# A planned order for the first 14 pairs of an attention and feed-forward kernel

## The chip, the cores and the metric

One core of one Trainium2 chip. The metric is the device time of one execution in microseconds, median of three runs.

## What is computed

Attention with a sliding window and a few sink columns, in 4 batches of 8 heads, 768 rows, head size 64; its output (3072 x 512) goes through a feed-forward layer of width 2048. Inputs are float32 (the weights arrive as 8-byte floats).

```python
scores = scale * np.matmul(q, k.transpose(0, 1, 3, 2))
keep = is_sink | in_window            # pos < n_sink, or 0 <= i - j < window
scores = np.where(keep, scores, -1000000000.0)
a = softmax(scores)                   # with 1e-9 added to the sum
x = (a @ v), heads side by side       # 3072 x 512
h = x @ w_in
g = h * np.clip(h + 3.0, 0.0, 6.0) / 6.0
out = g @ w_out
```

## The kernel before

The rows of a batch are cut into three blocks of 256 (u = 0, 1, 2). A *unit* is one block of one batch, all heads; there are 12, and the four with u = 0 come first. A *pair* is two heads of a unit, so four pairs make a unit and there are 48 (index s). Pairs 0 to 11 (`plain`, NF32 = 12) are multiplied in float32; from pair 12 on each operand is split into a high and a low float32r part.

A pair goes through these steps: `A_kq`, `A_v` load keys, queries and values (SP's queue); `C_score` multiplies on TensorE (PE) into four PSUM banks (tile `sp`); `C_mask` on VectorE (DVE) adds the mask and takes the row minimum (four cells, narrow 128 and wide 256 columns, into tile `Ph`, minimum in `nb`); `C_exp` on ScalarE (ACT) makes exponentials and row sums (four cells); `C_sum` inverts the sums; `C_norm` multiplies each cell by them; `D_pt` transposes on PE (tile `pt`), `D_out` copies the result to `pf` on ACT; `E_av` multiplies by the values on PE (tile `av`); `E_out` splits the result into `xh` (ACT) and `xl` (DVE).

The feed-forward layer of a unit needs its four pairs. It has 32 steps on PE: `ffn1` (L534) for each of 8 column blocks i and two halves, 12 matmuls into `hps`; `ffn2` (L564) for each i and two row tiles, 6 matmuls into `o`. Between them ACT makes the relu, DVE the product, ACT or DVE the high part `gh` and DVE the low part `g`. The weights come in 32 parts of 512 KB (`load_part`, L134): a load on SP's queue, two ACT operations and two DVE operations that turn 8-byte floats into 4-byte ones (tiles `st`, `wt`), then the high part on ACT (`wih`, `woh`) and the low part on DVE (`wil`, `wol`). Three `st` buffers and one `vs` buffer hold loaded parts.

The program has two halves. In the loop over `range(FROM)` (L667, FROM = 14) each turn s issues the steps of the string ORDER for pairs s, s-1 and s-2, some weight parts (WN), and feed-forward steps (`drain`) as far as the weights have come; the framework orders each engine's instructions there. From L717 on the order is written by hand (`manual_schedule`, the strings STAGES): each turn runs eight stages of a pair, and after each stage one feed-forward step. `keep_busy` (L77) issues matmuls without use, 50 calls in all, each two instructions in the trace.

Ahead of the pairs DVE makes the masks from `n_sink` and `window`, which are loaded by two small DMAs (L87, L88), in a chain of thirteen operations (L90 to L121); `later_constants` (L183) makes the masks for u > 0 on GpSimd (POOL).

The normalisation alternates (NORM0 = "DADA": narrow cells on DVE, wide cells on ACT); the high part of a weight is always on ACT (WHI = "A").

Of the kernel before, what the change touches and what calls it, by code (L numbers as in the profile page):

```python
# [18 lines left out]
P = 128  # L19
# [4 lines left out]
WARM = (10, 16, 4)  # L24
# [20 lines left out]
def attn_ffn_kernel(ctx: ExitStack, tc: tile.TileContext, qx, kx, vx, vfx, vsx, n_sink, window, w_in, w_out, out):  # L45
# [14 lines left out]

    rel = work.tile([P, 2, 256], F32, tag="gf", name="rel", bufs=2)
# [21 lines left out]
    keep_busy(WARM[0])  # L83
# [23 lines left out]
    own, prev, snk = relf[:, P:2 * P], relf[:, 2 * P:3 * P], colf[:, P:2 * P]  # L107
    tmpm = colf[:, 2 * P:3 * P]
    nc.vector.tensor_scalar(out=own, in0=relf[:, 0:P], scalar1=win_f, scalar2=None, op0=ALU.is_lt)
    nc.vector.scalar_tensor_tensor(out=own, in0=relf[:, 0:P], scalar=0.0, in1=own, op0=ALU.is_ge, op1=ALU.mult)  # L110
    nc.vector.tensor_scalar(out=prev, in0=relf[:, 0:P], scalar1=float(P), scalar2=win_f, op0=ALU.add, op1=ALU.is_lt)
    nc.vector.tensor_scalar(out=snk, in0=colf[:, 0:P], scalar1=ns_f, scalar2=None, op0=ALU.is_lt)

    def bias_from(dst, keep, engine=nc.vector):
        engine.tensor_scalar(out=dst, in0=keep, scalar1=-1.0, scalar2=BIG, op0=ALU.add, op1=ALU.mult)

    nc.vector.tensor_tensor(out=tmpm, in0=own, in1=snk, op=ALU.max)
    bias_from(m_00, tmpm)
    nc.vector.tensor_tensor(out=tmpm, in0=prev, in1=snk, op=ALU.max)
    bias_from(m_01[:, 0:P], tmpm)  # L120
    bias_from(m_01[:, P:2 * P], own)  # L121

# [6 lines left out]
    WHI, WLO = "A", "D"  # L129
# [4 lines left out]
    def load_part(hi, lo, src, rows, at):  # L134

        def like(t):
            return t.rearrange("p (a b) -> p a b", a=rows)

        if not wide:
            st = like(work.tile([P, 512], F32, tag="st", name="st", bufs=3))  # L140
            nc.sync.dma_start(out=st, in_=src)
            split_parts(nc, hi, lo, st, nc.scalar, nc.vector)
            return

        tag, bufs = ("vs", 1) if at % 4 == 3 else ("st", 3)
        st = work.tile([P, 512, 2], I32, tag=tag, name="st", bufs=bufs)
        it = work.tile([P, 512], I32, tag="wt", name="wt", bufs=3)
        nc.sync.dma_start(out=like(st.rearrange("p n w -> p (n w)")), in_=src.bitcast(I32))
        low, high = st[:, :, 0], st[:, :, 1]
        ft = it.bitcast(F32)  # L150


        nc.scalar.activation(out=ft, in_=high.bitcast(F32), func=AF.Abs, scale=2.0 ** -112)  # L153

        nc.scalar.activation(out=low, in_=low.bitcast(U32), func=AF.Copy, scale=2.0 ** -29 * (1 - 2.0 ** -18),  # L157
                             bias=7.5 * 2.0 ** -18 - 0.5)
        nc.vector.scalar_tensor_tensor(out=low, in0=high, scalar=-2 ** 31, in1=low,  # L159
                                       op0=ALU.bitwise_and, op1=ALU.bitwise_or)  # L160
        nc.vector.scalar_tensor_tensor(out=it, in0=it, scalar=3, in1=low,
                                       op0=ALU.logical_shift_left, op1=ALU.bitwise_or)
        copy_r(nc, weng(WHI, at), hi, like(ft))
        weng(WLO, at).tensor_tensor(out=lo, in0=like(ft), in1=hi.bitcast(F32), op=ALU.subtract)

    def load_w_in(i, c):
        cs = slice(2 * c, 2 * c + 2)
        load_part(WIH[i][:, cs, :], WIL[i][:, cs, :], w_in[i, :, cs, :], 2,
                  4 * i + c)

    def load_w_out(i, c):
        cs = slice(c, c + 1)
        load_part(WOH[i][:, cs, :], WOL[i][:, cs, :], w_out[i, :, cs, :], 1,
                  4 * i + 2 + c)


# [6 lines left out]
    def later_constants():  # L183

        bias_from(m_t0[:, 0:P], prev, nc.gpsimd)
        bias_from(m_t0[:, P:2 * P], own, nc.gpsimd)
        bias_from(m_t0[:, 2 * P:W2], snk[:, 0:SK], nc.gpsimd)
# [39 lines left out]
    NF32 = 12  # L227
    PFE = "AA"
# [13 lines left out]
    def A_v(s, planned=False):  # L242
# [13 lines left out]
        if not planned:  # L256
            A_split(s)
# [44 lines left out]
    PTAGS = [("pl", 2), ("pl", 2), ("Pt", 1)]  # L302

# [6 lines left out]
    def C_score(s, planned=False):  # L310
# [4 lines left out]
        if not plain(s):  # L315
            d["P"] = work.tile([P, 2, 2, WP], F32, name="Pt", bufs=1)
        d["sp"] = []
        for t, (k0c, w, m) in enumerate(spans(u)):
# [12 lines left out]
            if not planned:  # L331
                C_mask(s, t)
        if u and not planned:
            merge(s)

    def C_mask(s, t):
# [4 lines left out]
        for g in range(2):  # L341
            i = 2 * g + t
            if t == 0 and plain(s):
                tag, bufs = PTAGS[(2 * s + g) % len(PTAGS)]
                d[f"P{g}"] = work.tile([P, 3 * P], F32, tag=tag, name="Ph", bufs=bufs)
            d["min"] = nc.vector.tensor_tensor_reduce(out=cell(s, g, t, 0, w), in0=sp[g][:, 0:w], in1=m[:, 0:w],  # L346
                                                      scale=-SCALE, scalar=3.0e38, op0=ALU.add, op1=ALU.min,
                                                      accum_out=d["nb"][:, i:i + 1])
# [7 lines left out]
    NORM0, NORM = "DADA", "AAAA"  # L356

    def norm(e, blk, c):
        if e == "A":
            nc.scalar.mul(out=blk, in_=blk, mul=c)  # L360
        elif e == "D":
            nc.vector.tensor_scalar(out=blk, in0=blk, scalar1=c, scalar2=None, op0=ALU.mult)
        else:
            nc.gpsimd.tensor_scalar(out=blk, in0=blk, scalar1=c, scalar2=1.0, op0=ALU.mult, op1=ALU.mult)

# [3 lines left out]
    def C_exp(s, planned=False):  # L369
        d = st_[s]  # L370
        for i in range(4):
            blk = cell(s, i // 2, i % 2, *live(s)[i % 2])
            d["exp"] = nc.scalar.activation(out=blk, in_=blk, func=AF.Exp, scale=-1.0,  # L373
                                            bias=d["nb"][:, i:i + 1], accum_out=d["sm"][:, i:i + 1])
        if not planned:
            C_sum(s)
# [6 lines left out]
    def C_norm(s, planned=False):  # L383
        u = pus[s][1]
        d = st_[s]
        for i in range(4):
            blk = cell(s, i // 2, i % 2, *live(s)[i % 2])
            norm((NORM0 if s < START else NORM)[i], blk, d["rc"][:, i:i + 1])
        if not planned:
            C_sinks(s)  # L390
# [11 lines left out]
    def D_pt(s, h, planned=False):  # L402
# [12 lines left out]
        if not planned:  # L415
            D_part(s, h)
            D_out(s, h)
            if h == 1:
                D_sinks(s)
# [11 lines left out]
    def D_out(s, h):  # L431
        u = pus[s][1]
        d = st_[s]
        w = 4 * P if u else 3 * P
        pt = d[f"pt{h}"]
        if plain(s):
            ph = work.tile([P, 512], F32, tag="ph", name="pf")
            copy_r(nc, {"D": nc.vector, "A": nc.scalar}[PFE[h]], ph[:, 0:w], pt[:, 0:w])
            d[f"pt{h}"] = ph
            return  # L440
        ph = work.tile([P, 512], F32R, name="ph")
        pl = work.tile([P, 512], F32R, name="pl")
        split_parts(nc, ph[:, 0:w], pl[:, 0:w], pt[:, 0:w], nc.scalar, nc.vector)
# [9 lines left out]
    def E_av(s, h, planned=False):  # L453
# [34 lines left out]
        if h == 1:  # L488
            E_x(s)
            if not planned:  # L490
                E_out(s)
# [9 lines left out]
    def E_out(s):  # L501
        b, u, p = pus[s]
        d = st_[s]
        xh, xl = xt[(b, u)][p]
        if plain(s):
            acc = d["av"][:, 0, :]
            copy_r(nc, weng(XHF, p), xh, acc)
            nc.vector.tensor_tensor(out=xl, in0=acc, in1=xh.bitcast(F32), op=ALU.subtract)  # L508
            return
        for h in range(2):  # L510
            E_low(s, h)
            E_sum(s, h)
        E_split(s)
# [20 lines left out]
    def ffn1(x, i, pool, psum, half, state, tag):  # L534
# [12 lines left out]
        if half == 1:  # L547
# [5 lines left out]
            def activate():  # L553
                nc.scalar.activation(out=gf, in_=hp, func=AF.Relu, bias=three, scale=1.0)  # L554
# [363 lines left out]
```

## Time and profile before

| | us |
|---|---|
| median of 3 runs (722.68 to 724.12) | 723.58 |
| the profiled execution | 722.53 |
| its span, first to last instruction | 720.8 |

| engine | busy us | share of the span |
|---|---|---|
| PE, matmuls | 707.2 | 98% |
| PEld, weight loads | 626.3 | 87% |
| DVE | 504.5 | 70% |
| ACT | 451.4 | 63% |
| POOL | 5.0 | 1% |

Times are microseconds from the start of the span. A busy PE is not a PE at full flow: matmuls overlap, and the time from one start to the next tells more than the busy time. PEclk is the clock granted to TensorE, 1.00 being full. 49.45 MB are moved in the span.

### The profile page before, as it was taken

The page shows a single profiled execution, that of the slowest core. Times are in us where ns is not written, and L with a number is a line of the kernel's source. Part 1 is how long each engine was busy: PE and PEld are TensorE (multiplying, and loading weights), DVE is VectorE, ACT ScalarE, POOL GpSimd, SP SyncE. Part 2 cuts the span into 40 slices and gives each one's busy share as a digit, 9 for nine tenths or more (in the row PEclk, how much of TensorE's full clock was granted, in tenths as well). Part 3 has the DMA queues.
Part 4 walks back from the last instruction along what each step waited for, and adds up shares of the span by engine and source line. Part 5 has one row for each costly group of instructions (what it writes and reads, how often), then busy time and mean ns, then how long its engine had stood idle before and what let it go on. Part 6 is the DMA issues. An engine that isn't in the chain of part 4 may idle for free.

```text
span 720.8 us, 13229 instructions
## 1 busy us (share of the span) xinstructions
PE 707.2 (98%) x4948; PEld 626.3 (87%) x4948; DVE 504.5 (70%) x1322; ACT 451.4 (63%) x1179; POOL 5.0 (1%) x19
## 2 busy tenths in 40 slices
PE   8999999999999999999999999999999999999996
PEld 7777897889889898989898989898988898889995
DVE  5799997346578777877777777777777777775221
ACT  6999886447657656665666566656665665655222
POOL 2000000000000000000000000000000000000000
PEclk9999999999999999999999999999999999999999
DMA  6667561110211111112112111100121101100000
GB/s 240 194 199 238 188 206 61 52 52 1 64 31 60 42 49 60 31 59 68 30 31 85 35 38 60 60 32 30 60 66 32 60 30 61 60 13 1 30 1 35
DMA packets 29481, 49.45 MB, mean 69 GB/s; under 512 B 3552, under 2 KB 20448, under 8 KB 29408
## 3 DMA queue, kind: packets, MB, share of 16 engines
q1 hardware_dynamic: 29264, 48.51, 20.9%
q8 instruction: 41, 0.67, 0.4%
q14 instruction: 32, 0.26, 0.1%
q10 hardware_dynamic: 144, 0.00, 0.0%
HBM read 42.21 MB, written 6.29 MB: 67 GB/s over the span
## 4 chain that ended last, share of the span: by engine, by line
PE 89%; ACT 6%; DVE 3%; DMA 1%; issue 1%; ACTq 0%; DVEq 0%; SPq 0%
PE o L572 37%; PE hps L545 36%; PE av L486 7%; PE sp L329 6%; PE pt L410 3%; ACT Ph L373 2%; ACT wt L153 1%; ACT Ph L360 1%; ACT pf L35 1%; ACT st L157 1%; DMA raw<-in_n_sink_dram 1%; DMA st<-in_w_out_dram 1%; DVE st L159 1%; PE spt L412 1%; ACT wih L35 0%
## 5 line engine op out<-in xcount | busy, mean ns | idle before, releaser
L545 PE MATMUL hps<-xh,wih 128*128 128x256 f32 x768 | 222.5, 290 | 2.0 <-ACT wih L35 1.4
L545 PE MATMUL hps<-xh,wil 128*128 128x256 f32 x768 | 217.0, 283 | 0.0
L545 PE MATMUL hps<-xl,wih 128*128 128x256 f32 x768 | 216.5, 282 | 0.1
L572 PE MATMUL o<-woh,gh 128*128 128x512 f32 x384 | 156.1, 407 | 1.3 <-DVE gh L41 1.3
L572 PE MATMUL o<-woh,g 128*128 128x512 f32 x384 | 151.6, 395 | 0.0
L572 PE MATMUL o<-wol,gh 128*128 128x512 f32 x384 | 151.1, 393 | 0.0
L545 PEld LDWEIGHTS hps<-xh,wih 128*128 128x128 f32 x768 | 144.8, 189 | 3.7 <-ACT wih L35 1.7
L545 PEld LDWEIGHTS hps<-xl,wih 128*128 128x128 f32 x768 | 145.0, 189 | 0.9 <-DVE xl L508 0.3
L545 PEld LDWEIGHTS hps<-xh,wil 128*128 128x128 f32 x768 | 144.7, 188 | 0.8 <-DVE nb L346 0.7
L35 ACT ACTIVATE ph<-pm 128x512 fp32r<-128x512 f32 x64 | 40.5, 632 | 108.5 <-DVE pm L427 108.5
L555 DVE SCALAR_TENSOR_TENSOR gf<-gf,hps 128x512 f32<-128x512 f32 x96 | 65.7, 684 | 55.0 <-ACT gf L554 54.6
L554 ACT ACTIVATE gf<-hps,three 128x512 f32<-128x512 f32 x96 | 65.6, 683 | 56.5 <-PE hps L545 56.4
L559 DVE TENSOR_TENSOR g<-gf,gh 128x512 fp32r<-128x512 f32 x96 | 66.4, 691 | 37.6 <-ACT gh L35 35.1
L572 PEld LDWEIGHTS o<-woh,gh 128*128 128x128 f32 x384 | 72.2, 188 | 18.4 <-issue 3.3
L572 PEld LDWEIGHTS o<-woh,g 128*128 128x128 f32 x384 | 72.1, 188 | 17.8 <-DVE g L559 0.7
L572 PEld LDWEIGHTS o<-wol,gh 128*128 128x128 f32 x384 | 72.4, 189 | 11.3 <-issue 0.3
L30 DVE TENSOR_TENSOR pl<-pm,ph 128x512 fp32r<-128x512 f32 x64 | 44.3, 692 | 44.7 <-ACT ph L35 44.7
L35 ACT ACTIVATE gh<-gf 128x512 fp32r<-128x512 f32 x80 | 50.1, 626 | 26.1 <-DVE gf L555 25.9
L373 ACT ACTIVATE Pt<-Pt,nb 128x144 f32<-128x144 f32 (+2 forms) x144 | 58.7, 409 | 2.2 <-DVE nb L346 1.0
L519 ACT COPY tmp<-av 64x256 f32<-64x256 f32 x72 | 26.5, 368 | 35.6 <-PE av L486 35.1
L346 DVE CUSTOM_DVE_ANT_0 Pt<-sp,m_t 128x272 f32<-128x272 f32 x128 | 48.5, 435 | 0.0
L360 ACT ACTIVATE Pt<-Pt,rc 128x144 f32<-128x144 f32 (+2 forms) x144 | 48.2, 408 | 0.5 <-DVE rc L381 0.5
(99 smaller groups left out, 979.3 us busy)
## 6 DMA issues: line engine op xcount, KB each, us to landing
st<-in_w_in_dram SPq DMA_DIRECT2D x16, 512.0 KB, 3.9
st<-in_w_out_dram SPq DMA_DIRECT2D x16, 512.0 KB, 4.7
kr<-in_kx_dram SPq DMA_DIRECT2D x32, 200.0 KB, 2.6
qr<-in_qx_dram SPq DMA_DIRECT2D x48, 128.0 KB, 2.8
out_dram<-ost SPq DMA_DIRECT2D x24, 256.0 KB, 2.2
vr<-in_vx_dram SPq DMA_DIRECT2D x32, 192.0 KB, 2.4
VF<-in_vfx_dram SPq DMA_DIRECT2D x12, 256.0 KB, 3.4
kr<-in_kx_dram SPq DMA_DIRECT2D x16, 128.0 KB, 3.1
```

The lines of the kernel that those rows point to most:

```text
L30: lo_engine.tensor_tensor(out=lo, in0=src, in1=hi.bitcast(F32), op=ALU.subtract)
L35: nc.scalar.mul(out=out, in_=src, mul=scale)
L329: nc.tensor.matmul(out=sp[g][:, 0:w], lhsT=l[gs], rhs=r[gs], start=(j == 0), stop=(j == len(terms) - 1))
L346: d["min"] = nc.vector.tensor_tensor_reduce(out=cell(s, g, t, 0, w), in0=sp[g][:, 0:w], in1=m[:, 0:w], scale=-SCALE, scalar=3.0e38, op0=AL ...
L360: nc.scalar.mul(out=blk, in_=blk, mul=c)
L373: d["exp"] = nc.scalar.activation(out=blk, in_=blk, func=AF.Exp, scale=-1.0, bias=d["nb"][:, i:i + 1], accum_out=d["sm"][:, i:i + 1])
L486: nc.tensor.matmul(out=o, lhsT=l, rhs=r, start=(j == 0 and (h == 0 or not plain(s))), stop=(j == len(seq) - 1 and (h == 1 or not plain(s))))
L545: nc.tensor.matmul(out=hp[:, half, :], lhsT=l, rhs=r, start=(j == 0), stop=(j == n - 1))
L554: nc.scalar.activation(out=gf, in_=hp, func=AF.Relu, bias=three, scale=1.0)
L555: nc.vector.scalar_tensor_tensor(out=gf, in0=gf, scalar=6.0, in1=hp, op0=ALU.min, op1=ALU.mult)
L559: eng(GLO, state["n"] * NP).tensor_tensor(out=g, in0=gf, in1=gh.bitcast(F32), op=ALU.subtract)
L572: nc.tensor.matmul(out=acc, lhsT=l[:, f, ts_], rhs=r[i][:, f, :], start=(i == 0 and f == 0 and j == 0), stop=(i == NFP - 1 and f == 1 and ...
```

## The change

A planner runs while the program is built. `first_tasks` lists all work of pairs 0 to 13 (C, D and E up to pair 12, or 11 for E), of the 32 weight parts and of the feed-forward steps of units 0 and 1 as tasks with an engine, a cost, what they wait for, a due number and the buffers that they take and give. `in_order` lets four engines choose, each time one is free, the ready task with the lowest due number for which buffers are there; the order that comes out is issued as it is, with all four engines under `manual_schedule` from the start of the program. Tasks of engine `"*"` go to ACT or DVE, whichever is free first: the normalisations `n`, the high parts of weights `wh` and of activations `h`. Where PE has nothing and the plan's time is below QUIET, one matmul without use (`idle`) is put in. After the plan the loop over STAGES goes on from pair 14 as before, with `A_kq(14)` and unit 2 queued.

The mask chain prepares a position tile that needs no loaded value ahead of the loads, keeps the biases themselves, and has seven operations behind the loads; both small loads are now on ACT's queue. Even pairs put both heads' cells in one `Pt` tile, odd ones in two `pl` tiles (before they went round over three).

```diff
+PART_DUE = (5.4, 14.1, 33.8, 61.6, 65.3, 70.3, 72.6, 72.7, 75.9, 78, 80, 86.7, 102.5, 103.4, 105.5, 115, 115.2, 116.3,
+            118.3, 119.3, 120.2, 122.7, 123.4, 124.1, 124.2, 124.4, 141.9, 161.5, 187.6, 205, 220.3, 236.5)
+LEAD = {"kq": 39.1, "v": 38.1, "w": 38.8}
+QUIET = 30.0
+ROOM = {"kq": 2, "V": 2, "vr": 1, "split": 1, "bank": 7, "pl": 2, "Pt": 1, "ph": 2, "st": 3, "vs": 1, "wt": 3, "gf": 2,
+        "gh": 2, "x0": 2, "x1": 2, "x2": 2, "x3": 2}
+def first_tasks():
+    def add(name, eng, cost, after, due, takes=(), gives=(), lag=0.12):
+    add("mask", "DVE", 5.0, [], -100)
+    for s in range(PAIRS):
+        d = 10 * s
+        add(f"kq{s}", "SP", 0.95, [], d - LEAD["kq"], ("kq",))
+        add(f"v{s}", "SP", 0.47, [], d - LEAD["v"], ("V",) if f32 else ("V", "vr"))
...
+        hold = ("pl", "pl") if f32 and s % 2 else ("Pt",)
+        add(f"C{s}", "PE", 0.8 if f32 else 1.0, start, d, ("bank",) * 4 + hold, ("kq",) if f32 else ("split",), 0.35)
+        for t in range(2):
+            for h in range(2):
+                add(f"t{s}.{t}{h}", "DVE", 0.345 if t else 0.21, [f"C{s}", "mask"], d + 0.1, (), ("bank",))
+                add(f"x{s}.{t}{h}", "ACT", 0.49 if t else 0.385, [f"t{s}.{t}{h}"], d + 0.2)
+        add(f"c{s}", "DVE", 0.41, [f"x{s}.{t}{h}" for t in range(2) for h in range(2)], d + 0.3, lag=0.1)
+        for h in range(2):
+            for t in range(2):
+                add(f"n{s}.{t}{h}", "*", (0.41, 0.27) if t else (0.3, 0.2), [f"c{s}"], d + 0.4 + 0.01 * h)
+            add(f"D{s}.{h}", "PE", 0.4, [f"n{s}.0{h}", f"n{s}.1{h}"] + [f"D{s}.0"] * h, d + 0.5,
...
+        if f32:
+            add(f"E{s}.0", "PE", 0.68, [f"o{s}.0", f"v{s}"], d + 0.7, ("bank", f"x{s % 4}"), ("ph",))
+            add(f"E{s}.1", "PE", 0.68, [f"o{s}.1", f"E{s}.0"], d + 0.7, (), ("ph", "V"))
...
+    for k in range(32):
+        d = PART_DUE[k]
+        add(f"w{k}", "SP", 0.47, [], d - LEAD["w"], (room,))
+        add(f"wa{k}", "ACT", 0.56, [f"w{k}"], d + 0.1, ("wt",))
...
+        add(f"wh{k}", "*", (0.54, 0.336), [f"wd{k}"], d + 0.4)
+        add(f"wl{k}", "DVE", 0.605, [f"wh{k}"], d + 0.5, (), ("wt",))
+    for n in range(2):
+        for i in range(8):
+            d = 1000 + 100 * n + 5 * i
+            add(f"F{n}.{i}.0", "PE", 1.42, xs + before + [f"wl{4 * i}", f"wl{4 * i + 1}"], d, ("bank",))
+            add(f"r{n}.{i}", "ACT", 0.57, [f"F{n}.{i}.1"], -50, ("gf",))
...
+            add(f"G{n}.{i}.0", "PE", 1.4, before + [f"g{n}.{i}", f"wl{4 * i + 2}", f"wl{4 * i + 3}"], d + 1.5,
...
-    nc.sync.dma_start(out=raw[:, 1, :], in_=window.bitcast(I32).partition_broadcast(P))
+    nc.scalar.dma_start(out=raw[:, 1, :], in_=window.bitcast(I32).partition_broadcast(P))
-    rawf = const.tile([P, 2, 2], F32, name="rawf")
-    nc.vector.tensor_copy(out=rawf, in_=raw)
...
+    own = m_01[:, P:2 * P]
+    beyond(own, causal, win_f)
+    or_sink(m_00, own)
+    beyond(ahead, shifted, win_f)
+    or_sink(m_01[:, 0:P], ahead)
+    beyond(m_t0[:, 2 * P:W2], colf[:, 0:SK], ns_f)
...
+    PLAN[0] = "tasks"
+    later_constants()
+    for name, e, _ in in_order(first_tasks()):
+        do(name, e)
+    A_kq(FROM)
+    ffn_queue(2)
+    PLAN[0] = "steps"
+    for s in range(FROM, NS + 2):
+        for steps in STAGES:
+            stage(s, steps)
             drain(1)
             tick()
```

## Rows read from the trace of the kernel before

**Rows 1.** Busy time by stretch: length; PE, PEld, DVE, ACT, POOL; PEclk, DMA, GB/s.
```profile
8.40:66.75 58.35, 52.95 (x354) 42.99 (x352) 49.62 (x162) 56.95 (x159) 0.19 (x1) 1.00 0.69 219
66.75:159.05 92.30, 91.26 (x576) 79.17 (x576) 65.59 (x149) 63.04 (x140) 0.95 (x1) 1.00 0.36 116
159.05:714.90 555.85, 555.85 (x3979) 497.46 (x3978) 386.00 (x996) 329.53 (x879) 0.00 (x0) 1.00 0.13 43
```

**Rows 2.** Timeline of PE at 159 us: start, length, engine, line, operation, tiles.
```profile
159.07 0.96 PE L329 MATMUL sp<-kt,qt 64*128 64x128 f32 x12
```

**Rows 3.** PE's instructions by line, 0 to 159.05 us: count, busy, mean ns, idle before.
```profile
L545 PE MATMUL hps<-xh,wih 128*128 128x256 f32 x132 | 38.2, 291 | 2.0 <-ACT wih L35 1.4 <-ACT xh L35 0.7
...
L572 PE MATMUL o<-woh,gh 128*128 128x512 f32 x64 | 26.7, 417 | 1.3 <-DVE gh L41 1.3
```

**Rows 4.** Chain of work, PE at full flow: start, length, what.
```profile
115.70 2.85 PE hps L545 x24
...
119.21 2.79 PE o L572 x12
```

**Rows 5.** Timeline of PE, 62 to 65 us: one run of D, C, E.
```profile
62.11 0.82 PE L410 MATMUL pt<-ident_r,Ph 128*128 128x128 f32 x6
62.86 0.93 PE L329 MATMUL sp<-kr,qr 64*128 64x128 f32 x8
63.71 1.57 PE L486 MATMUL av<-pf,VF 128*128 128x256 f32 x8
65.05 0.36 PE L545 MATMUL hps<-xh,wih 128*128 128x256 f32 x1
```

**Rows 6.** PE's instructions by line, 0 to 31 us.
```profile
L81 PE MATMUL idle<-rel 128*128 128x128 f32 x100 | 14.3, 306 | 1.1 <-POOL rel L65 1.1
L486 PE MATMUL av<-pf,VF 128*128 128x256 f32 (+1 forms) x31 | 6.7, 342 | 0.0
L329 PE MATMUL sp<-kr,qr 64*128 64x128 f32 (+1 forms) x40 | 5.6, 354 | 0.1
L410 PE MATMUL pt<-ident_r,Ph 128*128 128x128 f32 x24 | 4.2, 289 | 1.3 <-DVE Ph L362 1.2
```

**Rows 7.** PE's instructions by line, 31 to 66.75 us.
```profile
L545 PE MATMUL hps<-xh,wih 128*128 128x256 f32 x28 | 8.5, 303 | 2.0 <-ACT wih L35 1.4 <-ACT xh L35 0.7
...
L486 PE MATMUL av<-pf,VF 128*128 128x128 f32 (+1 forms) x35 | 6.7, 331 | 0.0
L329 PE MATMUL sp<-kr,qr 64*128 64x128 f32 (+1 forms) x32 | 5.4, 363 | 0.6 <-ACT pf L35 0.6
L572 PE MATMUL o<-woh,gh 128*128 128x512 f32 x10 | 4.1, 409 | 1.3 <-DVE gh L41 1.3
```

**Rows 8.** Chain of work to 125 us: DVE and ACT on it.
```profile
4.90 0.18 DVE rawf L90
...
8.17 0.06 DVE Ph L346
...
20.00 1.75 ACT Ph L373 x8
...
22.27 0.91 ACT Ph L360 x2
...
28.46 0.27 ACT xh L35
28.73 0.81 ACT pf L35 x2
...
45.19 0.33 DVE gh L41
...
54.25 0.52 ACT wih L35
...
103.78 0.61 DVE wt L161
```

**Rows 9.** Waits of SP's queue: waiter, releaser, us, times, longest.
```profile
SPq L148 <- DVE wt L161: 44.4, 23, 5.4
```

More of the change, by code (lines that the diff above doesn't have):

```diff
@@ new lines, in in_order @@
+def in_order(tasks):
+    room = dict(ROOM)
+    engines = ("PE", "ACT", "DVE", "SP")
+    free = dict(PE=5.5, ACT=2.9, DVE=1.0, SP=0.8)
+    then = {name: [] for name in tasks}
+    left, at = {}, {}
+    for name, task in tasks.items():
+        left[name] = len(task[2])
+        at[name] = 0.0
+        for a in task[2]:
+            then[a].append(name)
+    coming = [(0.0, k, name) for k, name in enumerate(tasks) if not left[name]]
+    heapq.heapify(coming)
+    freed, marks, order, ready = [(QUIET, 0, ("bank",))], sorted({QUIET, *free.values()}), [], []
+    count, wire = len(tasks), 0.0
+    while marks:
+        now = heapq.heappop(marks)
+        while marks and marks[0] <= now + 1e-9:
+            heapq.heappop(marks)
+        while coming and coming[0][0] <= now + 1e-9:
+            ready.append(heapq.heappop(coming)[2])
+        while freed and freed[0][0] <= now + 1e-9:
+            for r in heapq.heappop(freed)[2]:
+                room[r] += 1
+        moved = True
+        while moved:
+            moved = False
+            for k, e in enumerate(engines):
+                if free[e] > now + 1e-9:
+                    continue
+                best = None
+                for name in ready:
+                    task = tasks[name]
+                    if task[0] == e or (task[0] == "*" and 1 <= k <= 2):
+                        if all(room[r] >= task[4].count(r) for r in task[4]) and (best is None or task[3] < tasks[best][3]):
+                            best = name
+                if best is None:
+                    if k == 0 and now < QUIET and not any(tasks[n][0] == "PE" and t < now + 0.25 for t, _, n in coming):
+                        order.append(("idle", e, now))
+                        free[e] = now + 0.224
+                        heapq.heappush(marks, free[e])
+                    continue
+                _, cost, _, _, takes, gives, lag = tasks[best]
+                ready.remove(best)
+                for r in takes:
+                    room[r] -= 1
+                cost = cost if isinstance(cost, float) else cost[k - 1]
+                free[e] = end = now + cost
+                order.append((best, e, now))
+                if e == "SP":
+                    wire = max(wire, now + (2.8 if now < 4.5 else 1.5)) + (1.6 if best[0] == "w" else 0.8)
+                    end, lag = wire + 0.7, 0.1
+                count += 1
+                if gives:
+                    heapq.heappush(freed, (end, count, gives))
+                    heapq.heappush(marks, end)
+                heapq.heappush(marks, free[e])
+                for nxt in then[best]:
+                    left[nxt] -= 1
+                    at[nxt] = max(at[nxt], end + lag)
+                    if not left[nxt]:
+                        count += 1
+                        heapq.heappush(coming, (at[nxt], count, nxt))
+                        heapq.heappush(marks, at[nxt])
+                moved = True
+    assert {o[0] for o in order} >= set(tasks), [n for n in tasks if n not in {o[0] for o in order}][:20]
+    return order
@@ L58, in attn_ffn_kernel @@
     ps = fast.enter_context(tc.tile_pool(name="ps", bufs=8, space=PSUM))
+    ET = mybir.EngineType
+    fixed = ExitStack()
+    fixed.enter_context(tc.manual_schedule(engines={ET.PE, ET.Activation, ET.DVE, ET.SP}))
     rel = work.tile([P, 2, 256], F32, tag="gf", name="rel", bufs=2)
@@ L136, in like @@
         def like(t):
             return t.rearrange("p (a b) -> p a b", a=rows)
+        tag, bufs = ("vs", 1) if k % 4 == 3 else ("st", 3)
+        if wide:
+            st = work.tile([P, 512, 2], I32, tag=tag, name="st", bufs=bufs)
+            nc.sync.dma_start(out=like(st.rearrange("p n w -> p (n w)")), in_=src.bitcast(I32))
+        else:
+            st = work.tile([P, 512], F32, tag=tag, name="st", bufs=bufs)
+            nc.sync.dma_start(out=like(st), in_=src)
+        parts[k] = (hi, lo, like, st)
@@ L240, in A_kq, with A_v @@
         st_[s].update(kr=kr, qr=qr)
-    def A_v(s, planned=False):
+    def A_v(s):
         b, u, p = pus[s]
@@ L316, in C_score @@
             d["P"] = work.tile([P, 2, 2, WP], F32, name="Pt", bufs=1)
+        elif s % 2:
+            d["P0"], d["P1"] = (work.tile([P, 3 * P], F32, tag="pl", name="Ph") for h in range(2))
+        else:
+            both = work.tile([P, 2, 3 * P], F32, tag="Pt", name="Ph", bufs=1)
+            d["P0"], d["P1"] = both[:, 0, :], both[:, 1, :]
         d["sp"] = []
@@ L330, in C_score, with C_mask @@
                                      stop=(j == len(terms) - 1))
[L331 to L336, printed above, removed]
+    def C_mask(s, t, heads=(0, 1)):
         b, u, p = pus[s]
@@ L340, in C_mask @@
         k0c, w, m = spans(u)[t]
-        for g in range(2):
+        for g in heads:
             i = 2 * g + t
[L343 to L348, printed above, removed]
+            nc.vector.tensor_tensor_reduce(out=cell(s, g, t, 0, w), in0=sp[g][:, 0:w], in1=m[:, 0:w],
+                                           scale=-SCALE, scalar=3.0e38, op0=ALU.add, op1=ALU.min,
+                                           accum_out=d["nb"][:, i:i + 1])
     def merge(s):
@@ L600, in attn_ffn_kernel, with post @@
     PLAN = [False]
-    def post(ticks, what):
-        if PLAN[0]:
+    def post(ticks, *what):
+        if PLAN[0] == "steps":
             due.append([ticks, what])
-        else:
-            what()
+        elif not PLAN[0]:
+            for w in what:
+                w()
     def tick():
@@ L645, in attn_ffn_kernel @@
-    PRE = 0
-    for _ in range(PRE):
-        w_order.pop(0)()
-    A_kq(0)
-    A_kq(1)
-    B_k(0)
-    B_q(0)
-    def slot_E(s, h, planned=False):
-        if 0 <= s < NS:
-            E_av(s, h, planned)
-            b, u, p = pus[s]
-            if h == 1 and p == NP - 1:
-                r0 = b * S + u * UT
-                dsts = [out[r0 + P * tt:r0 + P * (tt + 1), :] for tt in range(2)]
-                queues.append(ffn_steps(units.index((b, u)), xt[(b, u)], work, ps, ps, dsts, "bank"))
@@ L735, in stage @@
                 behind[step]()
-    ET = mybir.EngineType
-    with tc.manual_schedule(engines={ET.PE, ET.Activation, ET.DVE, ET.SP}):
-        PLAN[0] = True
-        for s in range(FROM, NS + 2):
-            for steps in STAGES:
-                stage(s, steps)
-                drain(1)
-                tick()
-        while any(queues) or due:
-            run_due()
+    PLAN[0] = "tasks"
[8 more added lines that the diff above has]
+            stage(s, steps)
             drain(1)
             tick()
+    while any(queues) or due:
+        run_due()
+        drain(1)
+        tick()
+    fixed.close()
     PLAN[0] = False
```

361 lines of the change are left out of this document (189 added, 172 removed).

## The prediction

> **What bounds the kernel now.** I read the busy time by stretch first, then TensorE's instructions with their counts, then the chain of work, and the waits of SyncE's queue last. The stretches [rows 1] say where to look: from 159.05 to 714.9 us PE is busy for 555.85 of 555.85 us, DVE for 386.0 and ACT for 329.5. Nothing can be won there but by less matmul work, and the change takes none away. Before that it is different: from 8.4 to 66.75 us ACT is busy 56.95 of 58.35 us (98%), DVE 49.6 (85%), PE 52.95 (91%), and the 91% flatters, as the next steps show.
>
> The border is well chosen. At 159.07 us PE starts the score matmuls of pair 13 [rows 2]; in both kernels that is the second step of the hand-staged loop, which the change leaves as it is. Up to there PE has run 132 of each of three kinds of `hps` and 64 of each of three kinds of `o` matmuls [rows 3]: 396 = 33 steps of `ffn1` with 12 each and 192 = 32 steps of `ffn2` with 6 each, that is units 0 and 1 whole and one step of unit 2. The new kernel plans units 0 and 1 whole, queues unit 2, and its loop takes one step before pair 13's scores too. So the two reach the same point with the same work done, and what follows, 722.53 - 159.07 = 563.46 us in the profiled execution, should stay. **The question is only how much earlier than 159.07 us pair 13's scores start.**
>
> How much of these 159 us is TensorE's own need? At full flow 24 `hps` matmuls take 2.85 us and 12 `o` matmuls 2.79 us [rows 4], so 1.425 a step of `ffn1` and 1.395 a step of `ffn2`. One pair of unit 0 to 2 costs, by start to start in one run of them [rows 5]: two transposes' groups D 0.75 us, scores C 0.85, attention times values E 1.34, together 2.94. Sum: 33 x 1.425 + 32 x 1.395 = 91.7; 12 pairs 35.3; scores and transposes of pair 12 about 1.6. That is 128.6 us of 159.07, so **30.5 us of PE time are lost**. Where: up to 31 us PE did 40/8 C, 24/6 D and 31/8 E [rows 6], worth 12.4 us, and 18.6 were lost (filled with 100 warming matmuls). From 31 to 66.75 us it did 82 `hps` (28 + 27 + 27; one row of the three stands), 29 `o` (10 + 10 + 9, likewise), 4 C, 35/8 E and four D [rows 7], worth 9.7 + 6.7 + 3.4 + 5.9 + 3.0 = 28.7: 7.0 lost. The other 92.3 us hold the remaining 87.5 of work: 4.8 lost.
>
> **The change part by part.** *Mask chain.* DVE starts it at 4.90 us and the first masked score at 8.17 [rows 8]: 3.27 us for some thirteen small operations on the way of the first pair. Seven are left behind the load (the position tile is prepared before it), so by the same mean of 0.25 about 1.75 us. The window's load moves from SP's to ACT's queue behind the other one, which costs perhaps 0.4 us; SP's first key load moves up by as much. First masked score near 7.0 us: 1.1 us won.
>
> The constants that POOL makes move ahead of the first pairs and lose their arithmetic; POOL is busy 0.2 us in the whole next stretch [rows 1], so they cost nothing, and would cost a late mask of pair 16 if POOL were not free.
>
> *One-source operations to the free engine.* Per pair ACT does eight exponential and accumulator instructions (1.75 us), two wide normalisations (0.91), two evictions (0.81) and the high part of x (0.27) [rows 8]: 3.74 us against PE's 2.94. The wide normalisations may now go to DVE. The trace doesn't show a 128x256 one there; the nearest are a copy of 128x512 on DVE, 0.33 us, and 0.455 for the same cell on ACT, so a cell costs at most 0.33 and a pair's ACT share can fall to 2.83. The high part of a weight (`wih`, `woh`) costs ACT 0.52 us and, as the same copy on DVE, 0.33. DVE pays for it, with three 0.61 us operations per weight part as it is, but it had 8.7 us free in the stretch in which ACT had 1.4. Evening out (57 + 49.6 with moves that get cheaper by a third) is worth about 4 us of this stretch; the ends are 0 (the planner finds no free slot) and 5.5.
>
> *The order.* This is the largest part. Up to 66.75 us ACT and DVE are handed weight parts and pairs alternately, so a pair takes some 5.4 us (8.17 to 31 us for a little over four) and of `av` matmuls, eight a pair, 31 + 35 had run by 66.75 us [rows 6, 7]: 8.25 pairs, so the second unit became ready just before. Until then PE has one unit to work on, and only as far as weights are split. The plan's due numbers put pairs 0 to 3 before all but two weight parts, one more part before pair 4, and pair 6 before the fourth; from then on weights feed two units at once, so each part gives PE 2.8 us of work for about 2.2 us of DVE time. I work it out with 3.8 us a pair (2.8 if ACT and DVE share perfectly, half a weight part more, a tenth for latencies; ends 3.0 and 5.4, the present pace). First masked score 7.0, way of one pair from there through its transposes 4.2 (1.75, 0.91, D 0.75, and an estimated 0.8 for masked scores and sums), three more pairs 11.4, evictions, E and the split of x 3.4 (0.81, 1.34, 0.27, 0.33 and some waiting): unit 0 ready at 26 us, where the first `hps` now runs after 31 [rows 6, 7]. PE did by then 4 pairs and 2.45 us of the next: 14.2, so 11.8 lost (ends 9.5 and 17.5). Unit 1 is ready four pairs and three parts (3 x 0.61 + 0.33 each on DVE) later, 26 + 15.2 + 6.5 = 47.7 us; in that time PE has the rest of pairs 4 to 7 (9.3), C of pair 8, and the first one to two whole steps of unit 0 (5.6 to 8.5): 17.5 of 21.7, 4 lost (ends 2 and 7). Behind it PE has two units in hand; I take 4.0 lost where it was 4.8 (ends 2 and 6). What is late next there is PE itself: DVE is busy 65.6 of 92.3 us [rows 1], so it can take the moved work.
>
> *Sum.* 11.8 + 4.0 + 4.0 = 19.8 against 30.5: 10.7 us. The profiled execution took 722.53, which gives 711.8; its own time lies 1.05 below the median of the three runs (723.58), on which the comparison goes, so I expect **713.0 us**. With all good ends 13.5 are lost (706.6), with all bad ones 30.5 (723.6).
>
> *The clock.* In the 58 us in which PE was fed worst it was granted 1.00 throughout, the level of 2.4 GHz [rows 1], with 100 warming matmuls up to 31 us and no wait longer than the 1.4 us for `wih` [rows 6, 7]. The plan warms only where it expects PE idle before its time 30. The Trainium skill, "TensorE: Matmul & The Clock Gate", section "HAM oscillation", says that gaps in the feed put PE back to half clock and that the next burst then starts cold; by it the change would risk something between 30 and 48 us. No stretch of this trace shows that, so the sum is without it; it is a rival below.
>
> **The rivals.** *The order goes stale.* From the first pair to the last step four engines now run in a fixed order made from fixed costs. Where ACT or DVE is later than planned, PE stands at a pair's D or E although `ffn` work lies ready behind it. For: the plan gives a wide exponential 0.49 and a narrow one 0.385, mean 0.437, just the trace's 1.75/4, without reserve. Against: its other costs agree with the rows too. With five such places a pair and 0.1 to 0.15 us each, ten pairs give back 5 to 7 us: 718.5 us.
>
> *The clock falls.* If in the gaps between 30 and 48 us PE drops to 1.2 GHz for a third of the 17.5 us of work there, that third takes twice as long, 5.8 us: 719 us.
>
> *Slower: loads behind loads.* SP issues the loads of pairs and weights in one fixed order now. Before, SP stood 23 times before a weight load because DVE had not yet released its buffer, 44.4 us in all, up to 5.4 at once [rows 9]. If, with pairs ahead of weights, a weight load stands so and a pair's key load lies behind it, the pair's C is late by as much, and everything behind C in PE's order with it. Two such waits of 5.4 us eat the gain; from the third on the kernel is slower: 3 x 5.4 = 16.2, 729 us. Against: the plan counts the same buffers, and SP can't be worse than late by what DVE is late.
>
> *No effect.* If the weights' end, not the pairs, sets when PE is full, the early gain is waited for again later: 723.5 us. Against it: after 66.75 us only 4.8 us are lost, and DVE is busy 71% [rows 1].
>
> **How the numbers follow.** Forecast (708 to 717 us) 0.61; stale order 0.17; clock 0.05; no effect 0.06; slower 0.11. A measurement of this kernel tells about 0.2%, 1.45 us, from no change. Faster: 0.61 + 0.17 + 0.05 = 0.83; within: 0.06; slower: 0.11. The range goes from the good ends, 706, to 721, which takes in the stale order and the clock and leaves out no effect, slower and the rest of the tails.
>
> **What would show it.** Right: pair 13's scores start near 148 us, with the same counts of `hps` and `o` before them; the first `hps` near 26 us instead of 31; the last pair of unit 1 done before 50; ACT and DVE both above 90% between 8 and 60 us; the first masked score near 7; from pair 13 on a stretch as long as before. The stale order would show as PE waits for `Ph`, `pf` or `nb` with the sum of several us; the clock as a granted value below 1.00; the loads as C waiting for `kr`. Wrong would be the whole frame if the stretch after pair 13 changed its length.

## The result, and the profile after

The changed kernel takes 713.56 us (median of 4 runs, 712.80 to 713.95), the kernel before 723.50 (4 runs); the ratio is 0.9862, 95% interval 0.9845 to 0.9879. That is 9.9 us less, where 10.6 were forecast. Its profiled execution took 712.8 us, with a span of 711.0.

By stretch (length; busy time of PE, PEld, DVE, ACT, POOL; clock, DMA share, GB/s), cut at pair 13's scores, and the timeline row that gives the cut:

```profile
8.40:66.75 58.35, 57.19 (x413) 48.73 (x413) 54.35 (x187) 56.83 (x165) 0.56 (x3) 1.00 0.69 222
66.75:149.10 82.35, 81.47 (x515) 71.79 (x513) 62.87 (x136) 59.41 (x127) 0.95 (x1) 1.00 0.40 127
149.10:705.10 556.00, 555.24 (x3979) 497.04 (x3978) 385.93 (x996) 330.13 (x880) 0.00 (x0) 1.00 0.14 44
```

```profile
149.14 0.96 PE L497 MATMUL sp<-kt,qt 64*128 64x128 f32 x12
```

Beside [rows 1, 2]: pair 13's scores start 9.93 us earlier, at 149.14 instead of 159.07, and from there to the end of the span it is 561.86 us, before it was 561.73. The whole gain lies ahead of that point. ACT is as busy up to 66.75 us as it was (56.83 against 56.95 us of 58.35), DVE 4.7 us busier, PE 4.2 us busier.

PE's instructions from 0 to 31 us and then from 31 to 66.75 us, by line (count, busy, mean ns, idle before):

```profile
L245 PE MATMUL idle<-rel 128*128 128x128 f32 x92 | 14.2, 311 | 1.1 <-POOL rel L229 1.1
L641 PE MATMUL av<-pf,VF 128*128 128x256 f32 (+1 forms) x32 | 6.8, 345 | 0.3 <-ACT pf L195 0.2
L497 PE MATMUL sp<-kr,qr 64*128 64x128 f32 (+1 forms) x48 | 5.8, 351 | 0.6 <-DMA qr<-in_qx_dram 0.6
L560 PE MATMUL pt<-ident_r,Ph 128*128 128x128 f32 x25 | 3.9, 281 | 0.8 <-DVE Ph L540 0.8
```

```profile
L692 PE MATMUL hps<-xh,wih 128*128 128x256 f32 x41 | 12.1, 295 | 0.0
...
L641 PE MATMUL av<-pf,VF 128*128 128x256 f32 (+1 forms) x32 | 6.9, 340 | 0.1
L560 PE MATMUL pt<-ident_r,Ph 128*128 128x128 f32 x30 | 5.1, 275 | 0.0
L497 PE MATMUL sp<-kr,qr 64*128 64x128 f32 (+1 forms) x40 | 4.6, 350 | 0.0
L724 PE MATMUL o<-woh,gh 128*128 128x512 f32 x10 | 4.3, 429 | 0.0
```

I price these counts as the prediction did. Up to 31 us: 6 C, 25/6 D, 4 E make 13.6 us of work, 17.4 lost (before [rows 6]: 18.6). From 31 to 66.75 us: 121 `hps` (41 + 40 + 40), 30 `o`, 4 E, 5 D, 5 C make 34.7, 1.0 lost (before [rows 7]: 7.0). The rest of the 128.6 us of work fills the 82.4 us up to 149.14 but for 2.1 (before 4.8). In all 20.5 us are lost; 19.8 were forecast. But they are not where I had put them: **the first 31 us gained 1.2 us, the 36 after them 6.0, the rest 2.7.**

The second unit is what came early. The E (attention times values) of pair 7, the last of unit 1, now ends at 51.28 us; before it ended at 65.28 [rows 5], and the forecast was 47.7.

```profile
49.56 1.72 PE L641 MATMUL av<-pf,VF 128*128 128x256 f32 x8
```

PE waits for hardly anything now; these are all its waits in the span (us in total, times, longest):

```profile
PE idle L245 <- POOL rel L229: 1.1, 1, 1.1
PE pt L560 <- DVE Ph L540: 0.8, 1, 0.8
PE o L724 <- DVE g L710: 0.7, 1, 0.7
PE sp L497 <- DMA qr<-in_qx_dram: 0.6, 1, 0.6
PE o L724 <- ACT gh L195: 0.2, 1, 0.2
PE av L641 <- ACT pf L195: 0.2, 1, 0.2
```

The `hps` waits for `wih` and `xh` [rows 7] are gone. The first pair's masks, by contrast, came later. The timeline of DVE and PE (start, length), and the chain's row for the load on which DVE waited:

```profile
6.64 0.16 DVE L259 SCALAR_TENSOR_TENSOR neg<-raw 128x2 f32<-128x2 int32 x1 [4.83 <-DMA raw<-in_window_dram]
...
8.77 0.28 DVE L507 CUSTOM_DVE_ANT_0 Ph<-sp,m 128x128 f32<-128x128 f32 x1
```

```profile
31.28 0.36 PE L692 MATMUL hps<-xh,wih 128*128 128x256 f32 x1
```

```profile
1.19 5.35 DMA raw<-in_window_dram
```

### The profile page after: what moved, and what is told of

The parts are those of the page before. It is cut to its first block, busy times and chain, and to the rows that moved or that the text cites. A ratio compares the mean times of both kernels' runs of the same rounds, so it can differ in the third digit from the quotient of the medians.

```text
span 711.0 us, 13205 instructions
## 1 busy us (share of the span) xinstructions
PE 700.6 (99%) x4940; PEld 623.6 (88%) x4940; DVE 505.4 (71%) x1327; ACT 447.7 (63%) x1171; POOL 4.9 (1%) x18
## 4 chain that ended last, share of the span: by engine, by line
PE 82%; ACT 7%; DVE 6%; DMA 3%; issue 1%; ACTq 0%; DVEq 0%; SPq 0%
PE o L724 34%; PE hps L692 33%; PE av L641 7%; PE sp L497 5%; PE pt L560 3%; ACT Ph L524 2%; DMA st<-in_w_out_dram 1%; DVE st L338 1%; DVE wt L341 1%; ACT wt L333 1%; ACT st L335 1%; ACT Ph L538 1%; DMA raw<-in_window_dram 1%; DVE wil L346 1%; DMA st<-in_w_in_dram 1%
## 5 line engine op out<-in xcount | busy, mean ns | idle before, releaser
L195 ACT ACTIVATE gh<-gf 128x512 fp32r<-128x512 f32 x91 | 56.9, 625 | 26.7 <-DVE gf L704 25.9
```

The lines of the kernel that those rows point to most:

```text
L195: nc.scalar.mul(out=out, in_=src, mul=scale)
```

## The experiments

All are compared with the kernel before on the same chip. The changed kernel ran again on two of the chips, with ratios 0.9877 (beside the hurried pairs and the two runs on the kernel before) and 0.9868 (beside the measured costs, the second run of the window's load and the old pace with engines pinned) after the first 0.9862; their mean, 0.9869, is the anchor below, and a difference of 0.001 is 0.7 us. The engines pinned, the old pace, the first run of the window's load and the run without idle matmuls have no changed kernel beside them on their chip. "Lost" is PE's lost time by the pricing above: up to 31 us / 31 to 66.75 / from there to pair 13's scores.

| kernel | ratio (95%) | pair 13's scores | lost |
|---|---|---|---|
| before | 1 | 159.07 | 18.6 / 7.0 / 4.8 |
| changed | 0.9862 (0.9845, 0.9879) | 149.14 | 17.4 / 1.0 / 2.1 |
| changed, second time | 0.9877 (0.9862, 0.9892) | 148.30 | 17.4 / 1.0 / 1.2 |
| changed, third time | 0.9868 (0.9853, 0.9883) | 149.12 | 17.4 / 1.0 / 2.1 |
| engines pinned | 0.9886 (0.9869, 0.9903) | 150.90 | 17.5 / 2.7 / 2.1 |
| old pace of weights | 0.9989 (0.9977, 1.0001) | 157.06 | 18.5 / 3.2 / 6.7 |
| old pace, engines pinned | 1.0012 (1.0003, 1.0021) | 159.84 | 17.5 / 4.5 / 9.2 |
| hurried first pairs | 0.9939 (0.9925, 0.9952) | 154.06 | 17.1 / 2.7 / 5.7 |
| window's load on SP | 0.9855 (0.9836, 0.9873) | 148.30 | 16.7 / 0.8 / 2.2 |
| the same again | 0.9860 (0.9845, 0.9875) | 149.91 | 17.5 / 1.6 / 2.1 |
| no planned idle matmuls | 0.9876 (0.9859, 0.9893) | 148.92 | 17.5 / 1.9 / 0.9 |
| measured costs | 0.9862 (0.9847, 0.9877) | 147.14 | 17.4 / 0.2 / 0.9 |
| before, two pairs on the way | 1.0003 (0.9994, 1.0013) | 160.50 | 18.6 / 7.0 / 6.3 |
| before, 8 high parts on DVE | 1.0096 (1.0078, 1.0113) | 165.91 | 18.3 / 8.3 / 10.7 |

From pair 13's scores to the end of the span it is 561.0 to 562.2 us in every one of them. The column "lost" shows the second regularity: whatever was changed, 16.7 to 18.6 us are lost up to 31 us. Each row of it is one profile.

### Order or engines: a table of four

Two edits to the planner's tasks, each alone and both together. Engines pinned:

```diff
-                add(f"n{s}.{t}{h}", "*", (0.41, 0.27) if t else (0.3, 0.2), [f"c{s}"], d + 0.4 + 0.01 * h)
+                add(f"n{s}.{t}{h}", "ACT" if t else "DVE", 0.41 if t else 0.2, [f"c{s}"], d + 0.4 + 0.01 * h)
...
-        add(f"wh{k}", "*", (0.54, 0.336), [f"wd{k}"], d + 0.4)
+        add(f"wh{k}", "ACT", 0.54, [f"wd{k}"], d + 0.4)
...
-            add(f"h{n}.{i}", "*", (0.536, 0.336), [f"s{n}.{i}"], -50, ("gh",))
+            add(f"h{n}.{i}", "DVE", 0.336, [f"s{n}.{i}"], -50, ("gh",))
```

> The changed kernel in which the planner may not choose engines: narrow normalisations and the high parts of activations on DVE, wide normalisations and the high parts of weights on ACT, as in the kernel before; due numbers and planner as they are. Theory of the prediction (evening out ACT and DVE is worth about 4 us): about 717.5. Rival (the gain is in the order; the plan moves only a few operations on balance): at most 1.5 us above 713.6.

This is not quite the kernel before: there, from pair 9 on, ACT makes all four normalisations of a pair, so 18 of the 52 up to pair 12 go to DVE, in the pinned run 26.

The weights' due numbers at the old pace:

```diff
+OLD_DUE = [10 * s - 5 for s, n in enumerate((0, 1, 1, 1, 1, 2, 2, 2, 3, 6, 6, 7)) for _ in range(n)]
...
-        d = PART_DUE[k]
+        d = OLD_DUE[k]
```

> The changed kernel with other due numbers for the weight parts: 1, 1, 1, 1, 2, 2, 2, 3, 6, 6, 7 parts behind pairs 0, 1, 2 and so on, the pace of the kernel before; free choice of engines and the planner stay. Theory (the gain is that pairs go ahead of weights, so that a second unit is in hand early): 5 to 8 us of the 9.9 us are lost, 719 to 722, and PE loses time between 31 and 67 us again (7 us in the kernel before, 1 in the changed one). Rival (a fixed order by a planner with engines chosen freely does it, whatever the due numbers): within 2 us of 713.6.

> The planner with the due numbers at the old pace of the weight parts and with the engines pinned as in the kernel before: what is left is that an order fixed by a planner stands where the framework ordered. If the order pairs before weights is the gain and the planner as such none: ratio 0.998 to 1.004, 721 to 725 us. If a planned order as such is worth something: below 0.995.

| ratio | engines free | engines pinned |
|---|---|---|
| pairs ahead of weights | 0.9869 | 0.9886 |
| old pace of weights | 0.9989 | 1.0012 |

Down a column the order counts 0.0120 and 0.0126, about 8.7 and 9.1 us of 722; along a row the free choice counts 0.0017 and 0.0023, 1.2 and 1.7 us, the first within the intervals. So the rival won in the pinned run, and the theory of the order in the other two. The second unit goes with it: at the old pace the E of pair 7 ends at 59.70 us (60.98 with the engines pinned), where the changed kernel has 51.28.

```profile
58.23 1.47 PE L642 MATMUL av<-pf,VF 128*128 128x256 f32 x8
```

With both undone the planned order stands at 1.0012: it brings no gain by itself, and neither do the new mask chain, POOL's order and the tiles, which this run has too. But part of what it loses is the clock. In its profile PE stood 1.75 and 3.09 us, took up work, and soon after was granted 0.50, the level of 1.2 GHz. There `hps` start every 0.213 us instead of 0.119, which in all costs about 3 us (an estimate from these spacings):

```profile
76.63 0.39 PE L693 MATMUL hps<-xh,wih 128*128 128x256 f32 x1 [1.75 <-DVE gf L705]
90.05 0.36 PE L693 MATMUL hps<-xh,wih 128*128 128x256 f32 x1 [3.09 <-ACT st L336]
```

```profile
78.00:81.00 3.00, 3.00 (x16) 3.00 (x15) 2.91 (x8) 2.93 (x6) 0.00 (x0) 0.50 0.25 90
82.00:86.00 4.00, 4.00 (x36) 4.00 (x36) 4.00 (x8) 4.00 (x9) 0.00 (x0) 1.00 0.16 66
```

So all this together might be worth up to 3 us where the clock holds, and the 1.7 us of the lower row can be the clock as well as the choice. The profile of the old pace has no such fall, but the mean clock of its twelve executions is 0.994 to 0.999, against 0.997 to 0.999 in the changed kernel: part of the 8.7 us may be the clock too, brought about by the waits of the slower order; how much was not measured.

One part of what I expected of the old pace was wrong: of its losses 3.2 us lie between 31 and 67 us and 6.7 behind them. Of the 6.7 one wait of `o` for `gh`, shortly ahead of pair 13's scores, makes 2.2; where the rest comes from stays open.

```profile
152.38 0.51 PE L725 MATMUL o<-woh,gh 128*128 128x512 f32 x1 [2.16 <-ACT gh L196]
157.06 0.96 PE L498 MATMUL sp<-kt,qt 64*128 64x128 f32 x12
```

### Hurrying the first unit

```diff
+        hold = ["x3.10", "x3.11"] if 2 <= k < 6 else []
-        add(f"wa{k}", "ACT", 0.56, [f"w{k}"], d + 0.1, ("wt",))
+        add(f"wa{k}", "ACT", 0.56, [f"w{k}"] + hold, d + 0.1, ("wt",))
```

and the same for `wb`.

> The changed kernel in which the weight parts 2 to 5 may not start on ACT before the wide exponentials of pair 3 are done; everything else is planned as before. My prediction had unit 0 ready at 26 us, but the first hps of the changed kernel starts at 31.28. Theory (ACT has no idle time between 10 and 60 us, so weight work taken out ahead of pair 3 is only owed later; the early PE loss can't be won back by hurrying pairs): the first hps comes 0.5 to 2 us earlier, PE loses more after it, and the time is 1 to 5 us above the changed kernel. Rival (weight parts ahead of pair 3 cost the first unit its early start, as my 3.8 us a pair supposed): the first hps comes 2 us or more earlier and the time falls by 1 us or more.

The first `hps` starts at 30.54 us instead of 31.29 in the changed kernel on the same chip, and pair 13's scores at 154.06 instead of 148.30; by the ratios it is 4.5 us slower (0.9939 against 0.9877).

```profile
30.54 0.37 PE L693 MATMUL hps<-xh,wih 128*128 128x256 f32 x1
```

The theory's numbers came: holding four weight parts back bought 0.75 us at the front (in one profile; the kernel of the next section differs by 1.5 us there from profile to profile) and was slower behind, with 2.7 and 5.7 us lost where the changed kernel beside it lost 1.0 and 1.2. Its reason, work that is owed later, does not cover all of that. Of the 5.7 us 2.2 are again a wait of `o` for `gh`, and about 1.5 the clock, which fell to 0.50 behind that wait (`o` start every 0.43 us instead of 0.233), though it had not behind the same wait at the old pace:

```profile
147.82 0.50 PE L725 MATMUL o<-woh,gh 128*128 128x512 f32 x1 [2.16 <-ACT gh L196]
```

And the E of pair 7 ends at 50.68 us here, as early as in the changed kernel: an early second unit alone is not enough for the gain.

### The place of the window's load

```diff
-    nc.scalar.dma_start(out=raw[:, 1, :], in_=window.bitcast(I32).partition_broadcast(P))
+    nc.sync.dma_start(out=raw[:, 1, :], in_=window.bitcast(I32).partition_broadcast(P))
```

> The changed kernel with the window's load back on SP's queue, ahead of the first key load; order and all else unchanged. In the changed kernel this load, second on ACT's queue, lands at 6.54 us and the first masked score starts at 8.77. Theory (the load's place in a queue delays the masks, and PE, which is short of work only up to about 31 us, carries the delay to the end): the load lands near 4.9, the first masked score starts near 7.0, the first hps comes 1 to 2 us earlier, and the median falls by 1.0 to 2.0 us below the changed kernel's 713.6. Rival (the pace of the first pairs is set elsewhere, by the loads of pair 2 or by ACT): the masks come earlier, pair 2's scores stay near 17 us, and the median stays within 0.7 us of 713.6.

> The changed kernel with the window's load on SP's queue once more, beside the changed kernel on one chip: masks 0.8 us earlier should come out as 0.8 us (ratio lower by 0.0011), if PE's lost time up to 31 us passes to the end; by the rival the two are alike.

The first masked score came at 7.98 and 8.05 us, 0.8 earlier, not the 1.8 that I expected: with one load on each queue both landed 4.9 to 5.2 us after their issue, where the kernel before has 3.9 to 4.1. And it bought nothing that can be told: ratios 0.9855 and 0.9860, and beside the second 0.9868 for the changed kernel. In the first profile pair 2's scores (16.28 us, 17.06 in the changed kernel) and the first `hps` are about 0.8 us earlier, in the second (17.95) both are later:

```profile
8.05 0.28 DVE L507 CUSTOM_DVE_ANT_0 Ph<-sp,m 128x128 f32<-128x128 f32 x1
```

```profile
30.48 0.36 PE L692 MATMUL hps<-xh,wih 128*128 128x256 f32 x1
32.02 0.36 PE L692 MATMUL hps<-xh,wih 128*128 128x256 f32 x1
```

By the ratios the first is 1.0 us below the anchor and the second 0.6 us below the changed kernel beside it, both within the intervals. Neither theory nor rival is decided: whether earlier masks bring the first unit forward stays open.

### The clock

The start of one line:

```diff
-            {"mask": lambda: None, "idle": lambda: keep_busy(1),
+            {"mask": lambda: None, "idle": lambda: None,
```

> The changed kernel without the 36 planned matmuls without use; the first 10 stay. Theory (the clock is kept up by them, as my rival on the clock has it): a granted clock below 1.00 in some stretch before 50 us and 2 to 6 us more than 713.6. Rival (the real matmuls between them are enough): the granted clock stays 1.00 and the time stays within 0.7 us of 713.6.

By stretch, without the planned matmuls (columns as above):

```profile
9.00:16.00 7.00, 5.71 (x22) 4.25 (x22) 5.44 (x25) 6.05 (x20) 0.20 (x1) 0.52 0.93 338
0.00:31.00 31.00, 22.29 (x124) 17.10 (x124) 21.96 (x95) 22.14 (x70) 3.96 (x17) 0.89 0.70 227
31.00:66.75 35.75, 35.03 (x249) 30.26 (x250) 34.29 (x101) 35.73 (x96) 0.00 (x0) 1.00 0.64 202
```

Half of each expectation came true. The granted clock did fall, to a mean of 0.89 up to 31 us with PE busy 22.29 of 31 us; nearly all of it lies between 9 and 16 us, and from 16 us on it was back at 1.00, the level of 2.4 GHz. But the time did not follow: 0.9876 against 0.9869, pair 13's scores at 148.92. My reading is that up to 31 us PE waits for others anyway (in this profile 4.4 us for `Ph`, 2.8 for `qr` and 1.1 for `pf`), so that a C or E at the lower clock is done in time; no run tests this by itself. The Trainium skill, "TensorE: Matmul & The Clock Gate", section "HAM oscillation", has gaps in the feed lower the clock; the run agrees in that, and shows that the time need not follow.

### Two parts alone in the kernel before

Even pairs on one `Pt` tile, odd ones on two `pl` tiles:

```diff
-            if t == 0 and plain(s):
-                tag, bufs = PTAGS[(2 * s + g) % len(PTAGS)]
-                d[f"P{g}"] = work.tile([P, 3 * P], F32, tag=tag, name="Ph", bufs=bufs)
...
+        elif s % 2:
+            d["P0"], d["P1"] = (work.tile([P, 3 * P], F32, tag="pl", name="Ph") for h in range(2))
+        else:
+            both = work.tile([P, 2, 3 * P], F32, tag="Pt", name="Ph", bufs=1)
+            d["P0"], d["P1"] = both[:, 0, :], both[:, 1, :]
```

> The kernel before with one part of the change alone: even pairs keep both heads' cells in one Pt tile and odd pairs in two pl tiles, so two whole pairs are on their way at once, where three half tiles went round before. I had priced this part at nothing. If the pace of the pairs was held back by these tiles, the first hps comes 1 to 3 us earlier and the time falls by 2 to 4 us. If ACT, busy 98%, sets the pace, the time stays within 1.5 us of the kernel before.

1.0003: nothing, as I had priced it (its one profile is 1.4 us later at pair 13's scores, with the clock at 0.50 from 113 to 116 us). And a share of the weights' high parts moved by hand:

```diff
-    WHI, WLO = "A", "D"
+    WHI, WLO = "AAAD", "D"
```

> The kernel before with one part alone: the high part of every fourth weight part on DVE instead of ACT (8 of 32), order as it was. By the prediction's term for the free engine (ACT 98% busy, DVE with 8.7 us to spare) ACT is relieved of 4 x 0.52 us up to 66.75 us and the time falls by 1.5 to 2.5 us. By the rival that the order is what counts: within 1 us of the kernel before.

Neither: it is 7 us slower. ACT is relieved indeed, but PE waits for DVE's normalisations and minima more than before (1.2 and 1.0 us in all):

```profile
PE pt L410 <- DVE Ph L362: 4.1, 4, 2.7
PE sp L329 <- DVE nb L346: 2.4, 1, 2.4
```

Toward the end of the longest of these waits the clock fell to 0.50, and the next D, C and E took 5.61 us from start to start where the kernel before needs 2.94 [rows 5]:

```profile
64.85 1.51 PE L410 MATMUL pt<-ident_r,Ph 128*128 128x128 f32 x6 [2.68 <-DVE Ph L362]
70.46 0.56 PE L545 MATMUL hps<-xh,wih 128*128 128x256 f32 x1
```

```profile
65.00:70.00 5.00, 5.00 (x20) 3.75 (x21) 3.64 (x14) 3.70 (x12) 0.00 (x0) 0.50 0.47 156
```

The framework orders anew when an engine changes, so this run does not tell the operation's own price from that of the order and of the clock; it does show that the same kind of move without a plan can cost several times what it brings in a plan.

### Costs nearer to the trace

The masks' cost 6.9 instead of 5.0, C 0.86, D 0.39, ACT 1% and DVE 0.5% dearer, the window's load on SP, and other numbers in PART_DUE found for these costs.

> The changed kernel with the planner's numbers brought nearer to the trace: the masks end at 7.9 instead of 6.0, scores 0.86 and a transposes' group 0.39, ACT 1% and DVE 0.5% dearer; the window's load on SP's queue; and other due numbers of the weight parts, found for these costs. Theory (PE follows the plan, and from 31 us on has work whenever the plan says so): pair 13's scores start near 146 us instead of 148.3 to 149.1, and the ratio to the kernel before is 0.982 to 0.984, some 2 to 3 us below the changed kernel. Rival (deviations on the chip eat so small a planned gain): 0.985 to 0.988, as the changed kernel.

Pair 13's scores start at 147.14 us, 1.2 to 2.0 earlier than in the changed kernel's three profiles, with 18.5 us lost instead of 19.7 to 20.5.

```profile
147.14 0.96 PE L502 MATMUL sp<-kt,qt 64*128 64x128 f32 x12
```

The ratio, 0.9862, doesn't tell it from the changed kernel beside it (0.9868). Between 31 and 147 us PE loses 1.1 us there, so nothing is left but the first 31. Whether the better plan is worth its one or two microseconds stays open.

## Why the prediction was right, step by step

**The frame** was right. The steps of `ffn1` and `ffn2` ahead of pair 13's scores are the same in both kernels (again 132 of each kind of `hps` and 64 of each kind of `o`), and what follows them stayed within 0.8 us of 561.73 us in all runs.

**The sum** was right, 20.5 us lost against 19.8, but all three of its terms were mis-sized, by +5.6, -3.0 and -1.9 us, and they cancelled. No run shows that they had to: over the kernels of the table the losses behind 31 us go from 1.1 to 19.0 us while those ahead of it stay within 2. That the sum came within 0.7 us was luck.

*Unit 0 ready at 26 us* was wrong: the first `hps` starts at 31.28, hardly other than before. By the terms of the sum 1.8 of the 5.3 us are the later masks (8.77 instead of 7.0), and 0.6 the way from the last transposes to the first `hps` (4.0 instead of 3.4). The rest, 2.9, is the step that failed most, the pace of 3.8 us a pair: from pair 0's transposes to pair 3's it was 14.3 us for three pairs, not 11.4.

```profile
11.84 1.11 PE L560 MATMUL pt<-ident_r,Ph 128*128 128x128 f32 x6 [0.84 <-DVE Ph L540]
26.44 0.82 PE L560 MATMUL pt<-ident_r,Ph 128*128 128x128 f32 x6
```

I had counted half a weight part beside a pair; by 31 us ACT had started five parts and made 22 cells' exponentials, five and a half pairs (before: five parts and 18 cells). The plan lets no engine wait: while a pair's next step isn't ready, a weight part or the next pair is begun. In that way no time of ACT is lost, but the first unit isn't hurried. My bounds for this term, 9.5 to 17.5 us lost, just hold the 17.4.

*The stretch behind it* was wrong the other way: of 7.0 lost I left about 4, and it lost 1.0. The likely reason, which no run tests by itself, is that what ACT and DVE had done ahead by 31 us was work in hand from then on; the run with the hurried pairs fits it, but has a wait and the clock in it too. *The rest* lost 2.1 where I took 4.

*The order as the largest part* was right: 8.7 to 9.1 us by the table of four, the clock's share included. The reason I gave fits the traces: unit 1 is complete 14 us earlier, from then on two units draw on each weight part, and PE loses 3.1 us after 31 instead of 11.8.

*One-source operations* were mis-sized: about 4 us forecast, ends 0 and 5.5, and 1.2 to 1.7 measured. The plan uses its freedom little. In the order that is issued, of 52 normalisations 28 go to DVE, where 18 went before (NORM0 holds up to pair 8 only); of 32 high parts of weights 9; and of 16 high parts of activations 11 go the other way, to ACT. Up to 66.75 us ACT is as full as it was; what it no longer does for weights it spends on further pairs. The price of a wide cell on DVE was right: 347 ns busy, where the copy of 128x512 that I took as its upper bound has 418 in the same trace.

*The mask chain* failed in its sign: 7.0 us was forecast, 8.77 came. The operations became cheaper as expected (2.13 us from the first to the first masked score, 3.27 before [rows 8]), but the load on which they wait landed at 6.54 us, and DVE began 1.7 us later than before; I had priced the load's move to ACT's queue at 0.4 us. The runs that move it back give 0.7 to 0.8 of the 1.7; the rest came with something else in the changed kernel. Whether the late masks cost time at the end can't be told from these runs.

**The rivals.** The stale order did not come: PE's waits for `Ph`, `g`, `gh` and `pf` come to 1.9 us in all. The clock stayed at 1.00 up to pair 13's scores in all three profiles of the changed kernel, where PE's longest wait is 1.1 us. The rival was a real one all the same: without the planned matmuls a fall cost nothing, but in the old pace with pinned engines, the hurried pairs and the run with 8 high parts on DVE it cost 1.5 us or more each, at or behind waits of 1.75 to 3.09 us. Loads behind loads did not come either. SP's longest wait behind a weight buffer is shorter than before [rows 9], and only the first C waits for a load (0.6 us, `qr`):

```profile
SPq L313 <- DVE wt L341: 41.8, 22, 4.2
```

## What to carry to other kernels

Where one engine is full in a start-up phase, ask first which of its work opens most work for the engine that bounds the whole: here pairs for a second unit ahead of further weights, since every weight part is then used twice. A sum over the whole phase held where the terms for its parts did not, but by luck, so check the parts. Look at the granted clock before you put down a slower run to its order: a wait of TensorE can cost a second time by the clock behind it. A count of what must be done up to a point that both kernels share made the forecast possible at all.

## What the hardware showed that I had not expected

A small load on ACT's queue behind another landed 5.35 us after its issue; in the kernel before, with one such load on each queue, they took 3.9 to 4.1, and in the changed kernel with that arrangement 4.9 to 5.2. In the changed kernel the first weight load is issued at 2.14 us rather than at 4.89, which may be why; it wasn't tried alone. And a clock that fell to 0.50 cost nothing that can be measured between 9 and 16 us, before the first `hps`, but about 3 us in the old pace with pinned engines, where work lay ready: `hps` started every 0.213 us there instead of every 0.119.
